# Rope attention and SoLU MLP on one core: the first tables and keys loaded and rotated in two column halves, with a new order of issue

## The chip, the cores and the metric

The kernel runs on one core of a Trainium2 chip. The metric is the device time of one execution in microseconds (us); the median of three timed runs stands for the kernel. A profile is taken of one further execution, and all rows below are of that one.

## The reference, cut to what matters

Rotary attention over 4 batches x 8 heads of 576 positions x 64, and then an MLP over the 2304 rows of 512 that the heads give together:

```
q_rot, k_rot = rotate(q), rotate(k)                      # x1*cos - x2*sin, x1*sin + x2*cos
attn = softmax(scale * q_rot @ k_rot.T) @ v              # per batch and head
h = x @ w_in                                             # 2304x512 @ 512x1024
solu = h * softmax(h);  ln = layernorm(solu) * g_ln
out = ln @ w_out                                         # 1024 -> 512
```

## The kernel before

**Tiling.** The 32 heads go as 16 pairs (P = 0 to 15): a pair's two heads lie in the two halves of the 128 partitions. `raw["k"]` and `raw["q"]` hold one pair as the chip loads it, 128 partitions x 2 planes x 576 columns: plane 0 is x, plane 1 is x with its halves swapped. The table `tabs` has the same shape (cosines, sines). A rotation is three operations (line 359, a helper that DVE or POOL runs): plane 0 times cosine, plane 1 times sine, and their sum into `rot`. Pairs 0 to 3 multiply `rot` in fp32; from pair 4 on each operand is split in a high and a low fp32r part, and the scores take three products.

**Stages of a pair.** `pair_tile(i)`, i = 0 to 3, makes the scores of 128 queries of both heads, called S P.i here (line 425), into two of the three two-bank buffers "D" of PSUM. Then `stats`: DVE takes the row maximum (line 405), ACT the exponential into `e` (line 407). The scores' buffer is free after the exponential. `turn_tile` transposes `e`, called T P.i.h for the head h: in pairs 0 to 3 on TensorE (line 489), from pair 4 on nearly always by DMA, out to `escr`, back into `e`, and then a DVE transposition in blocks into `ET` (line 510). `packed` makes the last 64 queries of both heads (S P.4, lines 452 to 461), and `av` multiplies with v (A P.r, line 564). After four pairs a batch is whole, and its 4 or 5 row tiles go through `front` (h, line 638) and `back` (o, line 711).

**The prologue** (`prologue`, line 729) loads table and pair 0 and rotates pair 0. The query goes in two column pieces, columns 0 to 191 first. `early` (line 721) issues matmuls without use on a constant tile: five of them ahead of the first scores, two after them. `weights` splits the two weight matrices in high and low parts (jobs w0 to w15, lines 809 to 828); its loads and operations lie among the first pairs.

**Order.** Every operation is added to a list with a number (`Plan.add`); `ORDER` is a hand-kept permutation of these numbers, and the program issues them in it. Every engine runs its own operations strictly in that order, and all loads and stores go through one queue, SP. `FLIP` holds the numbers of operations that run on their second engine (DVE in place of POOL or ACT, mostly, or POOL for DVE), `BUFS` the buffer of each use. Where an operation has to wait, all that stands behind it on its engine waits too.

The places that matter below, by the numbers of `ORDER`:

- Prologue: loads 12 to 18, rotations 23 to 33, first scores S 0.0 = 117.
- Pair 4: load of the pair-6 keys = 691 and queries = 692; `e` back from `escr` for T 4.0.1 = 702, its DVE transposition = 703.
- Pair 6: load of the pair-9 queries = 987; `e` back from `escr` for T 6.3.0 = 943, its DVE transposition = 944; the same two of T 6.0.1 = 899 and 900.

Of the kernel before, what the change touches and what calls it, by code (L numbers as in the profile page):

```python
# [32 lines left out]
    2, 12, 16, 13, 27, 14, 23, 17, 29, 15, 24, 3, 4, 5, 6, 7, 18, 26, 25, 28, 30, 32, 117, 126, 34, 38, 35,  # L33
    19, 31, 33, 118, 119, 127, 43, 44, 120, 36, 37, 39, 45, 47, 122, 123, 121, 1, 52, 53, 106, 128, 131,
    132, 20, 129, 130, 40, 124, 109, 125, 139, 140, 141, 108, 151, 154, 133, 56, 10, 155, 152, 46, 48, 135,
    107, 112, 134, 160, 136, 137, 163, 61, 158, 138, 153, 110, 142, 161, 9, 115, 143, 144, 49, 65, 111, 171,
    164, 172, 113, 54, 145, 146, 159, 70, 147, 148, 162, 55, 173, 41, 42, 149, 50, 179, 57, 116, 167, 168,
    201, 204, 114, 150, 62, 63, 58, 169, 170, 193, 205, 156, 174, 157, 175, 180, 202, 203, 210, 176, 178,
    177, 181, 182, 64, 165, 166, 79, 211, 206, 207, 213, 185, 214, 192, 208, 186, 209, 71, 72, 195, 196,
    197, 200, 194, 233, 234, 212, 221, 235, 222, 184, 183, 223, 236, 59, 187, 188, 217, 218, 51, 80, 66, 8,  # L40
    73, 237, 224, 242, 243, 244, 74, 215, 21, 216, 245, 189, 190, 238, 239, 75, 253, 81, 191, 254, 82, 240,
    246, 249, 67, 68, 83, 199, 60, 84, 88, 76, 283, 277, 250, 284, 241, 85, 225, 77, 219, 220, 278, 279,
    255, 227, 228, 229, 261, 262, 230, 231, 285, 286, 89, 263, 288, 69, 86, 90, 289, 226, 232, 287, 292,
    295, 251, 252, 97, 293, 296, 258, 260, 87, 78, 446, 247, 248, 294, 303, 98, 275, 282, 315, 318, 259,
    301, 302, 264, 290, 265, 256, 319, 324, 450, 267, 99, 257, 268, 291, 447, 274, 269, 270, 297, 100, 316,
    92, 327, 325, 328, 101, 266, 335, 304, 305, 298, 271, 448, 102, 198, 91, 276, 281, 272, 326, 329, 306,
    317, 336, 337, 330, 361, 373, 362, 93, 103, 104, 363, 364, 273, 456, 374, 320, 321, 343, 308, 280, 340,
    342, 341, 94, 486, 375, 376, 357, 105, 356, 307, 338, 339, 358, 371, 299, 377, 372, 300, 449, 382, 383,
    385, 457, 458, 359, 360, 322, 323, 95, 309, 96, 310, 22, 333, 334, 344, 345, 386, 311, 384, 312, 313,
    314, 346, 451, 452, 466, 393, 394, 395, 380, 396, 368, 405, 406, 487, 488, 348, 459, 489, 381, 347, 461,  # L50
    378, 460, 391, 379, 407, 331, 453, 408, 332, 392, 454, 414, 415, 417, 677, 409, 387, 388, 416, 350, 351,
    462, 418, 476, 349, 491, 389, 390, 490, 398, 676, 425, 463, 365, 693, 426, 427, 696, 697, 467, 682, 433,
    434, 694, 397, 681, 678, 468, 11, 477, 695, 399, 400, 401, 402, 492, 701, 403, 683, 493, 404, 528, 352,
    353, 354, 355, 470, 704, 419, 420, 410, 366, 411, 423, 496, 435, 529, 530, 691, 424, 478, 707, 705, 706,
    702, 412, 708, 494, 469, 471, 472, 479, 413, 531, 421, 436, 480, 717, 718, 500, 698, 481, 482, 495, 709,
    729, 730, 732, 692, 430, 699, 532, 679, 680, 703, 497, 498, 437, 684, 719, 367, 431, 712, 422, 499, 534,
# [12 lines left out]
    836, 819, 901, 640, 880, 889, 860, 861, 862, 809, 863, 562, 844, 563, 564, 881, 891, 892, 834, 902, 849,
# [874 lines left out]
```

## Time and profile before

| | |
|---|---|
| median of 3 runs | 445.88 us (445.01 to 448.03) |
| profiled execution | 447.05 us |
| its span, first to last instruction | 445.3 us |
| mean granted TensorE clock | 0.995 |
| busy: PE, DVE, ACT, POOL | 97%, 86%, 65%, 56% |
| moved by DMA | 109.29 MB, mean 245 GB/s |

A row of the timeline reads: start, duration, engine, line, operation, what it writes <- what it reads, shapes, count, and in brackets the engine's idle time before it and what ended that. PE is TensorE's matmuls, PEld its weight loads, SPq the issue of a DMA on the queue SP. A row of the windows gives the busy time of each engine in a stretch, the granted clock (1.00 is 2.4 GHz, 0.50 is 1.2 GHz), the busy share of the DMA engines and their rate.

### The profile page before, as it was taken

What the parts mean: (1) busy time and instruction counts of PE and PEld (TensorE: products, weight loads), DVE (VectorE), ACT (ScalarE), POOL (GpSimd) and SP (SyncE); (2) the same over time, 40 slices, a digit from 0 to 9 for tenths busy, and PEclk for the clock granted to TensorE, in tenths of its full rate; (3) what the DMA queues carried; (4) which work ended last, traced back from release to release, by engine and by line L of the source; (5) the groups of instructions that cost most, each with busy time, mean ns of one, the idle gap of its engine ahead of it and who ended that gap; (6) DMA issues with size and microseconds to landing.
All of it is one profiled execution on the core that took longest, in us unless ns stands there. A gap on an engine that the chain in (4) does not pass through costs nothing.

```text
span 445.3 us, 8147 instructions
## 1 busy us (share of the span) xinstructions
PE 431.1 (97%) x2658; PEld 312.9 (70%) x2658; DVE 382.7 (86%) x608; ACT 291.6 (65%) x646; POOL 250.2 (56%) x286
## 2 busy tenths in 40 slices
PE   7889999999999998999999999999999999999996
PEld 3465666777777685767677678777776776868885
DVE  3999989999999988888799899989899987865762
ACT  1989999999876764567465767576867545344431
POOL 2656766688889657375586577366747330303440
PEclk9999999999999998999999999999999999999999
DMA  7746575788899989998999999999999976534331
GB/s 254 270 164 217 167 222 178 234 257 298 248 311 306 266 263 277 296 282 248 321 315 275 292 346 288 295 302 283 270 282 292 311 223 214 173 106 165 118 142 48
DMA packets 93243, 109.29 MB, mean 245 GB/s; under 512 B 8464, under 2 KB 68752, under 8 KB 93200
## 3 DMA queue, kind: packets, MB, share of 16 engines
q1 hardware_dynamic: 93200, 108.76, 77.3%
q8 instruction: 21, 0.34, 0.3%
q14 instruction: 22, 0.18, 0.1%
HBM read 70.91 MB, written 37.82 MB: 244 GB/s over the span
## 4 chain that ended last, share of the span: by engine, by line
PE 71%; DMA 8%; DVE 5%; issue 4%; SPq 2%; POOL 2%; ACT 1%; DVEq 0%; POOLq 0%; ACTq 0%
PE pg L711 20%; PE pd L638 19%; PE pg L564 13%; PE pd L425 10%; PE pg L489 7%; DMA e<-escr 5%; PE pd L452 2%; DMA escr<-e 1%; DVE ET L510 1%; SPq L343 1%; DVE mx L405 1%; DMA wraw<-uscr 1%; PE pg L839 1%; DMA rscr<-rs 1%; POOL rawk L359 1%
## 5 line engine op out<-in xcount | busy, mean ns | idle before, releaser
L407 ACT ACTIVATE e<-pd,mx 128x576 f32<-128x576 f32 x132 | 97.4, 740 | 43.6 <-DVE mx L405 25.7
L510 DVE STREAM_TRANSPOSE ET<-e 128x512 f32<-128x512 f32 x90 | 99.7, 1132 | 5.6 <-DMA e<-escr 5.5
L405 DVE TENSOR_REDUCE mx<-pd 128x1 f32<-128x576 f32 x132 | 94.7, 742 | 9.8 <-PE pd L425 8.8
L564 PE MATMUL pg<-ET,vst 128*64 128x256 f32 (+1 forms) x512 | 70.4, 414 | 0.2 <-ACT ET L328 0.2
L703 POOL TENSOR_TENSOR lnl<-tb,lnh 128x512 fp32r<-128x512 f32 x26 | 33.7, 1297 | 46.7 <-ACT lnh L328 40.3
L638 PE MATMUL pd<-wih,xh 128*128 128x512 f32 x144 | 59.2, 411 | 0.0
L711 PE MATMUL pg<-woh,lnh 128*128 128x512 f32 x144 | 59.0, 410 | 0.0
L489 PE MATMUL pg<-idn,e 128*128 128x128 f32 (+1 forms) x308 | 54.7, 295 | 4.0 <-ACT EL L328 1.7
L489 PEld LDWEIGHTS pg<-idn,e 128*128 128x128 f32 (+1 forms) x308 | 40.8, 186 | 24.6 <-issue 6.4
L711 PE MATMUL pg<-woh,lnl 128*128 128x512 f32 x144 | 57.0, 396 | 0.0
L638 PE MATMUL pd<-wih,xl 128*128 128x512 f32 x144 | 56.9, 395 | 0.0
L711 PE MATMUL pg<-wol,lnh 128*128 128x512 f32 x144 | 56.9, 395 | 0.0
L638 PE MATMUL pd<-wil,xh 128*128 128x512 f32 x144 | 56.8, 395 | 0.0
L564 PEld LDWEIGHTS pg<-ET,vst 128*64 128x64 f32 x512 | 34.0, 137 | 24.9 <-issue 4.0
L693 DVE STREAM_TRANSPOSE tb<-wraw 128x512 f32<-128x512 f32 x36 | 38.4, 1096 | 1.1 <-DMA wraw<-uscr 1.1
L425 PE MATMUL pd<-kh,qh 64*128 64x288 f32 x192 | 34.7, 343 | 2.5 <-ACT e L407 1.6
L359 POOL TENSOR_TENSOR rawq<-rawq,tabs 128x576 f32<-128x576 f32 (+1 forms) x22 | 29.9, 1361 | 11.0 <-DMA rawq<-in_q_t_dram 10.8
L359 POOL TENSOR_TENSOR xl<-xT,xh 128x512 fp32r<-128x512 f32 x15 | 20.0, 1331 | 27.5 <-ACT xh L328 27.0
L328 ACT COPY ET<-pg 128x512 f32<-128x512 f32 x50 | 28.8, 584 | 9.9 <-PE pg L489 9.7
L359 POOL TENSOR_TENSOR rawk<-rawk,tabs 128x576 f32<-128x576 f32 x21 | 30.4, 1457 | 7.1 <-DMA rawk<-in_k_t_dram 7.0
L711 PEld LDWEIGHTS pg<-woh,lnh 128*128 128x128 f32 x144 | 27.1, 188 | 7.4 <-issue 1.8
L711 PEld LDWEIGHTS pg<-woh,lnl 128*128 128x128 f32 x144 | 27.1, 188 | 6.8 <-POOL lnl L703 0.3
(120 smaller groups left out, 891.9 us busy)
## 6 DMA issues: line engine op xcount, KB each, us to landing
escr<-e SPq DMA_DIRECT2D x90, 256.0 KB
e<-escr SPq DMA_DIRECT2D x90, 256.0 KB
uscr<-u SPq DMA_DIRECT2D x18, 512.0 KB
wraw<-uscr SPq DMA_DIRECT2D x18, 512.0 KB
rawk<-in_k_t_dram SPq DMA_DIRECT2D x15, 576.0 KB
rawq<-in_q_t_dram SPq DMA_DIRECT2D x15, 576.0 KB
vst<-in_v_t_dram SPq DMA_DIRECT2D x16, 320.0 KB
out_dram<-o SPq DMA_DIRECT2D x18, 256.0 KB
```

The lines of the kernel that those rows point to most:

```text
L328: nc.scalar.copy(o, i)
L359: add(*c[0], prio, lambda e: e.tensor_tensor(o, a, b, op=op), r, w, alt=c[1], two=True)
L405: add("dve", 672, t, lambda: nc.vector.tensor_reduce(mx[:, mcol:mcol + 1], buf(us)[:, :, 0:288], axis=AX.XY, op=ALU.max, negate=True), [sk ...
L407: add("act", 720, t, lambda: nc.scalar.activation(e.rearrange("p (z n) -> p z n", z=2), buf(us)[:, :, 0:288], AF.Exp, bias=mx[:, mcol:mcol ...
L425: nc.tensor.matmul(buf(us)[:, z, 0:288], a[rows, c0:c0 + 128], w[rows, 288 * z:288 * z + 288], start=(j == 0), stop=(j == len(terms) - 1))
L489: nc.tensor.transpose(dst, src, idn)
L510: add("dve", 1040, t, lambda: nc.vector.transpose(ET[r][:, h, :, q0:q0 + 128].rearrange("p m (a j) -> p j m a", j=4), e.rearrange("p (j b ...
L564: nc.tensor.matmul(buf(uy)[rows, 0:nq], vv[:, m, h, :], e, start=(m == 0), stop=(m == 4))
L638: nc.tensor.matmul(buf(uh)[:, z, :], a[:, c, :], w[:, c, HF * z:HF * z + HF], start=(c == 0 and j == 0), stop=(c == KC - 1 and j == 2))
L693: add("dve", 1050, tl, lambda z=z, turned=turned: nc.vector.transpose(turned().rearrange("p m (a j) -> p j m a", j=4), v[:, :, 128 * z:128 ...
L703: add(*c[0], tl, lambda e, hd=hd, ld=ld, turned=turned: e.tensor_tensor(ld, turned(), hd, op=ALU.subtract), [bk] + kl[0][z], kl[1][z], use ...
L711: nc.tensor.matmul(buf(uo), a[:, f, :], w[:, f, :], start=(f == 0 and j == 0), stop=(f == FC - 1 and j == 2))
```

## The change

Four edits of the code:

1. The table is loaded as two halves of columns (0 to 287, 288 to 575), each with both planes, and the keys of pair 0 likewise. Before, the table came as two planes, the keys as plane 0 whole and plane 1 in two halves. There are two loads of the table and two of the keys now, 1152 bytes in a row each; before two of the table and one of the keys with 2304 bytes in a row and two of the keys with 1152.
2. The keys are rotated in two halves of three operations each; before, plane 0 was multiplied in one operation of 576 columns.
3. S 0.0 is two operations, one for each half of the keys, and the first needs only the first half.
4. `ORDER`, `FLIP` and `BUFS` are replaced. Numbers from 118 on are one higher, since S 0.0 is two operations.

```diff
-        dma(-100, tabs[:, 0, :], tab[:, 0, :], nb, w=[("tab", 0)])
-        dma(-99, tabs[:, 1, :], tab[:, 1, :], nb, w=[("tab", 1)])
-        dma(-98.5, raw["q"][:, :, h0], q_t[0][:, :, h0], nb * 2 / 3, w=[("raw", "q", "a")])
-        dma(-98, raw["k"][:, 0, :], k_t[0][:, 0, :], nb, w=[("raw", "k", "c")])
         for z, x in enumerate(hs):
-            dma(-97, raw["k"][:, 1, x], k_t[0][:, 1, x], nb / 2, w=[("raw", "k", "s", z)])
+            dma(-100 + z, tabs[:, :, x], tab[:, :, x], nb, w=[("tab", z)])
+            if z == 0:
+                dma(-100, raw["q"][:, :, h0], q_t[0][:, :, h0], nb * 2 / 3, w=[("raw", "q", "a")])
+            dma(-99.5 + z, raw["k"][:, :, x], k_t[0][:, :, x], nb, w=[("raw", "k", "h", z)])
...
-        tt("dve", -80, a, a, tabs[:, 0, :], ALU.mult, S, [("raw", "k", "c"), ("tab", 0)] + kw, [("rp", "k", 0)])
         for z, x in enumerate(hs):
-            tt("dve", -79, s_[:, x], s_[:, x], tabs[:, 1, x], ALU.mult, S // 2, [("raw", "k", "s", z), ("tab", 1)] + kw, [("rp", "k", 1, z)])
-            tt("dve", -79, rot["k"][0][:, x], a[:, x], s_[:, x], ALU.add, S // 2, [("rp", "k", 0), ("rp", "k", 1, z)] + kw,
+            ky = [("raw", "k", "h", z), ("tab", z)] + kw
+            tt("dve", -79, a[:, x], a[:, x], tabs[:, 0, x], ALU.mult, S // 2, ky, [("rp", "k", 0, z)])
+            tt("dve", -79, s_[:, x], s_[:, x], tabs[:, 1, x], ALU.mult, S // 2, ky, [("rp", "k", 1, z)])
+            tt("dve", -79, rot["k"][0][:, x], a[:, x], s_[:, x], ALU.add, S // 2, [("rp", "k", y, z) for y in range(2)] + kw,
...
-            def S_op():
-                for z in range(2):
+            def S_op(zs=range(2)):
+                for z in zs:
...
+            if jt == 0:
+                for z in range(2):
+                    add("pe", 485, tau(P, 0) - 4, lambda z=z: S_op((z,)), [kk[z], q0k], sk + [("turn",)], use=(ua, ub), mode=1)
```

What the two lists say, read by operation and engine:

| place | before | after |
|---|---|---|
| SP, start | table plane 0, keys plane 1 first half, table plane 1, queries 0 to 191, keys plane 1 second half, keys plane 0, queries 192 on, w0, identity, w1, w2, keys of pair 1, v, queries of pair 1 | queries 0 to 191, table half 0, keys half 0, table half 1, keys half 1, queries 192 on, w0, identity, w1, keys of pair 1, queries of pair 1, w2, v |
| PE, start | 5 early, S 0.0, 2 early, T 0.0.0, S 0.1, T 0.0.1, S 0.2 | 5 early, S 0.0 in two, 2 early, S 0.1, T 0.0.0, T 0.0.1, S 0.2 |
| ACT, start | w0 (two operations), exponential S 0.0 first head, w1 (two), exponential S 0.0 second head | w0 (two), exponential S 0.0 first head, w1 (one), exponential S 0.0 second head, w1 (one) |
| SP, pair 4 | 691 (pair-6 keys), 702 (`e` of T 4.0.1), 2 stores and 4 small ones, 692 (pair-6 queries) | 692 (pair-6 keys), 693 (pair-6 queries), 703 (`e` of T 4.0.1) |
| DVE, pair 4 | maxima of S 4.2, transposition T 4.0.1, w13 (three operations) | maxima of S 4.2, w13 (three operations), transposition T 4.0.1 |
| SP, pair 6 | 987 (pair-9 queries), 943 (`e` of T 6.3.0) | 900 (`e` of T 6.0.1), 944 (`e` of T 6.3.0); 988 (pair-9 queries) stands later, see below |
| PE, S 6.3 to S 7.3 | the same operations but for one transposition that stands before or after five o products | |
| DVE, all | 590 operations of the list | 585 |
| PE, all | 638 operations of the list in 260 runs of one kind | 639 in 256 |

The lines of `ORDER` for pair 4 and pair 6 (not whole):

```diff
-    353, 354, 355, 470, 704, 419, 420, 410, 366, 411, 423, 496, 435, 529, 530, 691, 424, 478, 707, 705, 706,
-    702, 412, 708, 494, 469, 471, 472, 479, 413, 531, 421, 436, 480, 717, 718, 500, 698, 481, 482, 495, 709,
-    729, 730, 732, 692, 430, 699, 532, 679, 680, 703, 497, 498, 437, 684, 719, 367, 431, 712, 422, 499, 534,
...
-    919, 992, 987, 655, 973, 980, 953, 954, 1260, 960, 943, 600, 601, 961, 900, 886, 989, 990, 996, 999,
...
+    684, 405, 529, 530, 679, 692, 481, 480, 494, 411, 412, 356, 420, 421, 706, 424, 707, 425, 434, 693, 435,
+    413, 708, 709, 703, 436, 470, 472, 482, 718, 535, 536, 495, 414, 719, 720, 710, 370, 371, 431, 433, 501,
...
+    973, 960, 974, 975, 934, 651, 961, 937, 887, 1001, 993, 985, 1003, 900, 1002, 901, 944, 945, 1004, 1013,
+    1014, 585, 652, 653, 654, 655, 656, 600, 980, 1025, 657, 988, 1026, 994, 919, 976, 1027, 1261, 659, 921,
```

## Rows read from the trace of the kernel before

**Rows 1.** The page, part 1: busy time and instructions of every engine.
```profile
PE 431.1 (97%) x2658; PEld 312.9 (70%) x2658; DVE 382.7 (86%) x608; ACT 291.6 (65%) x646; POOL 250.2 (56%) x286
```

**Rows 2.** Windows, 20 to 100 us: PE, PEld, DVE, ACT, POOL, clock, DMA share, GB/s.
```profile
20.00:100.00 80.00, 76.39 (x533) 50.75 (x533) 76.76 (x142) 74.44 (x169) 52.99 (x40) 1.00 0.64 205
```

**Rows 3.** Timeline of the first 18 us: rotations, first scores, first maxima and exponentials.
```profile
6.14 0.46 DVE L359 TENSOR_TENSOR rawk<-rawk,tabs 128x288 f32<-128x288 f32 x1 [4.76 <-DMA tabs<-in_tab_dram]
...
6.76 1.38 POOL L359 TENSOR_TENSOR rawq<-rawq,tabs 128x192 f32<-128x192 f32 x2 [6.33 <-DMA rawq<-in_q_t_dram]
...
8.02 0.76 DVE L359 TENSOR_TENSOR rawk<-rawk,tabs 128x576 f32<-128x576 f32 x1 [0.32 <-DMA rawk<-in_k_t_dram]
8.22 1.00 POOL L359 TENSOR_TENSOR rotq<-rawq 128x192 f32<-128x192 f32 x1
8.81 1.10 DVE L359 TENSOR_TENSOR rotk<-rawk 128x288 f32<-128x288 f32 x2
...
9.68 1.24 PE L425 MATMUL pd<-rotk,rotq 64*128 64x288 f32 x8 [0.88 <-DVE rotk L359]
...
10.05 1.03 DVE L359 TENSOR_TENSOR rawq<-rawq,tabs 128x384 f32<-128x384 f32 x2
...
10.85 1.98 PE L725 MATMUL pg<-lnh 128*128 128x512 f32 x4
11.00 1.42 DVE L405 TENSOR_REDUCE mx<-pd 128x1 f32<-128x576 f32 x2
...
11.49 0.68 ACT L817 ACTIVATE wraw<-wraw 128x512 int32<-128x512 uint32 x1 [9.49 <-DMA wraw<-in_w_in_dram]
...
12.62 0.72 ACT L407 ACTIVATE e<-pd,mx 128x576 f32<-128x576 f32 x1
...
14.17 1.24 PE L425 MATMUL pd<-rotk,rotq 64*128 64x288 f32 x8
...
17.14 1.24 PE L425 MATMUL pd<-rotk,rotq 64*128 64x288 f32 x8 [0.97 <-ACT e L407]
```

**Rows 4.** Windows of 2 us, the first loads; columns as in Rows 2.
```profile
4.00:6.00 2.00, 2.00 (x4) 0.81 (x3) 0.00 (x0) 0.00 (x0) 0.00 (x0) 1.00 0.95 278
```

**Rows 5.** Waits of PE, 100 to 445 us: us in total, times, longest.
```profile
PE pd L425 <- ACT e L407: 1.6, 1, 1.6
```

**Rows 6.** Timeline, 159 to 170 us: queue SP, DVE and PE around T 6.3.0.
```profile
159.53 0.59 SPq L343 DMA_DIRECT2D rawq<-in_q_t_dram  x1
160.24 0.37 SPq L343 DMA_DIRECT2D e<-escr  x1
...
167.31 1.15 DVE L510 STREAM_TRANSPOSE ET<-e 128x512 f32<-128x512 f32 x1 [2.10 <-DMA e<-escr]
...
169.99 0.40 PE L425 MATMUL pd<-kh,qh 64*128 64x288 f32 x1 [1.55 <-ACT e L407]
```

**Rows 7.** Windows after that stall, and after the idle time at 17 us.
```profile
170.00:175.00 5.00, 5.00 (x31) 3.75 (x33) 3.83 (x8) 2.82 (x8) 3.29 (x3) 0.66 1.06 340
...
18.00:20.00 2.00, 1.55 (x12) 1.05 (x8) 1.93 (x6) 1.66 (x5) 1.53 (x2) 1.00 0.36 140
```

**Rows 8.** Timeline, 83 to 93 us: queue SP, POOL and DVE around T 4.0.1.
```profile
83.41 1.55 POOL L359 TENSOR_TENSOR rotq<-rawq 128x576 f32<-128x576 f32 x1 [0.69 <-DVE rawq L359]
...
84.04 0.33 SPq L343 DMA_DIRECT2D e<-escr  x1
...
88.23 0.45 SPq L343 DMA_DIRECT2D rawq<-in_q_t_dram  x1
...
91.55 1.13 DVE L510 STREAM_TRANSPOSE ET<-e 128x512 f32<-128x512 f32 x1
```

**Rows 9.** Groups by line and shape, DVE, 15 to 100 us: busy us, mean ns of one.
```profile
L359 DVE TENSOR_TENSOR rawk<-rawk,tabs 128x576 f32<-128x576 f32 x7 | 5.9, 849 | 0.0
L811 DVE TENSOR_SCALAR xT<-xT 128x512 f32<-128x512 f32 x9 | 5.6, 625 | 0.0
...
L359 DVE TENSOR_TENSOR wil<-xT,wih 128x512 fp32r<-128x512 f32 x3 | 2.4, 789 | 0.0
```

More of the change, by code (lines that the diff above doesn't have):

```diff
@@ L32 @@
 ORDER = [
[127 rows of a table removed]
[127 rows of a table added]
 ]
 FLIP = {
[5 rows of a table removed]
[5 rows of a table added]
 }
 BUFS = (
-    "0010002110002111100112011101002001021000201100101211011000211110101010121010200100211100002011101221"
-    "0200102011001000121001212101111012010202100001210100101010111102120110211011010012111220012001110210"
-    "2112011120021101102121112101010110220002021100011211010101010000020011121200200212112121101220101001"
-    "02210112101211020021020011121011020002010000002200112110200201200121010"
+    "0011002101001211200111011201010001020012100120001011211001011021100010112101010100201011102001011012"
+    "1102011011010100102012020002001211001101202100100211202001001021020101201111110010011010210202012101"
+    "2102010120200001001221112121120012002000201002110012111212112010011221200100201212100121101201002011"
+    "10020102211011001101110101120010110000112121011002100010101210201210011"
 )
@@ L370, in rope @@
             e = eng[p]
-            tt(e, prio, a, a, tabs[:, 0, c0:c1], ALU.mult, n, [rk[0], ("tab", 0)], [pk[0]])
-            tt(e, prio, s_, s_, tabs[:, 1, c0:c1], ALU.mult, n, [rk[1], ("tab", 1)], [pk[1]])
+            tk = [("tab", 0), ("tab", 1)]
+            tt(e, prio, a, a, tabs[:, 0, c0:c1], ALU.mult, n, [rk[0]] + tk, [pk[0]])
+            tt(e, prio, s_, s_, tabs[:, 1, c0:c1], ALU.mult, n, [rk[1]] + tk, [pk[1]])
             tt(e, prio, o, a, s_, ALU.add, n, pk + rk, wk)
@@ L766, in turn_q @@
             ky = [("raw", "q", y)] + qw
-            tt("dve", p, a, a, tabs[:, 0, c], ALU.mult, n, ky + [("tab", 0)], [("rp", "q", 0, y)])
-            tt("dve", p, s_, s_, tabs[:, 1, c], ALU.mult, n, ky + [("tab", 1)], [("rp", "q", 1, y)])
+            tk = [("tab", 0)] + ([("tab", 1)] if y == "b" else [])
+            tt("dve", p, a, a, tabs[:, 0, c], ALU.mult, n, ky + tk, [("rp", "q", 0, y)])
+            tt("dve", p, s_, s_, tabs[:, 1, c], ALU.mult, n, ky + tk, [("rp", "q", 1, y)])
             tt("dve", p, rot["q"][0][:, c], a, s_, ALU.add, n, [("rp", "q", 0, y), ("rp", "q", 1, y)] + qw, [("rot", "q", 0, "ab".index(y))])
```

3 lines of the change are left out of this document (2 added, 1 removed), and 256 rows, old and new, of tables (FLIP, ORDER).

## The prediction

> **What bounds the kernel now.** First the page's busy times: TensorE is busy for 97% of the span, DVE for 86% [rows 1]. So the kernel is worth what TensorE does not spend, 445.3 - 431.1 = 14.2 us of the span, and what it spends slowly. Then the windows say where that idle time lies. From 20 to 100 us, which is pairs 0 to 3 and the weights, PE is idle for 80 - 76.39 = 3.6 us, DVE for 3.2 us, ACT for 5.6 us [rows 2]: three engines are nearly full, so an operation handed to one of them can lengthen that stretch, and an earlier start is soon eaten by whichever is fullest. After 100 us PE's list of waits has one that matters, 1.6 us in one piece for an exponential [rows 5]. The timeline shows its whole chain [rows 6]: a load of raw queries of 576 KB is issued at 159.53, the load of `e` for T 6.3.0 behind it at 160.24; DVE idles for 2.10 us until that lands and transposes at 167.31; the maxima of S 7.2 stand behind it on DVE, their exponentials on ACT behind them, and S 7.3 needs the buffer that these free. PE idles for 1.55 us to 169.99. The windows then show the second price: from 170 to 175 us the mean granted clock is 0.66 [rows 7], so 0.34 x 5 = 1.70 us are lost at the lower level of 1.2 GHz. An idle time of 0.97 us ahead of 17.14 [rows 3] was followed by a clock of 1.00 [rows 7]. The one stall therefore cost 1.55 + 1.70 = 3.25 us.
>
> **The start, edits 1 to 3.** Before, DVE waited for table plane 1 to 6.14 and for keys plane 0 to 8.02 [rows 3]. Ahead of the one and with it the queue had 288 + 144 + 288 = 720 KB, up to the other 1344 KB: 624 KB in 1.88 us, 332 KB a us. By the new order queries and both first halves make 768 KB, so the first keys are there at 6.14 + 48 / 332 = 6.28, and the table's first half (480 KB) at 5.42. All 1344 KB are still there at 8.02. POOL's query rotation took from 6.76 to 9.22, 2.46 us [rows 3], and now ends at 5.42 + 2.46 = 7.88. Three half operations on DVE take 0.46 + 0.46 + 0.55 = 1.47 us (0.55 is half of the 1.10 of the two sums): the first half is rotated at 7.75, the second at 8.02 + 1.47 = 9.49, where before it was 9.91. The early matmuls end at 9.68 - 0.88 = 8.80; the first part of S 0.0 follows at once and takes half of 1.24, 0.62; the second part starts at 9.5 and ends at 10.1, in place of 10.92. So the first scores are 0.8 us sooner. DVE then has the two query operations (1.03) and starts the first maximum at 10.5 rather than 11.00, 0.5 us sooner. There it ends: ACT runs two operations of w0 first, which waited for their load to 11.49, and the first exponential comes at 12.62, after them [rows 3]; the new order leaves these two ahead of it, and the bytes ahead of w0 are the same. What the order adds is that the second exponential stands ahead of one operation of w1 (0.68 sooner) and S 0.1 ahead of T 0.0.0: at 13.4, when the first exponential is done, rather than at 14.17. Bounds 0 to -0.8 us; ACT is the nearest limit and has 5.6 us of idle time in the next 80 [rows 2], so I take -0.3.
>
> With S 0.1 there, PE's two early matmuls end at 10.1 + 1.98 = 12.1 and PE idles for 1.3 us to 13.4, more than the 0.97 that kept the clock and less than the 1.55 that lost it. Price 0 to 1.7; I take 0, because here PE waits for ACT anyway.
>
> w2's load and that of v move behind both loads of pair 1, which wait for the rotations of pair 0; v is multiplied only with the first `av`, after four scores, and w2's operations stand later on ACT as well. I cost both at nothing; uncovered, it would be the 0.68 of one ACT operation.
>
> **Smaller pieces.** Rows of 2304 bytes become 1152: on average over these loads 1344 KB go from 896 to 1280 rows, 1536 to 1075 bytes. With 0.95 of the DMA engines' time used they moved 278 GB/s [rows 4]. From below: from 170 to 175 us, with stores of `e` in pieces of 512 bytes among the traffic, 340 GB/s were moved [rows 7], so a shorter piece need not cost. From above: if the rate fell with the length of a piece, the about 4.1 us of transfer to 8.02 grow by 0.43, +1.8 us. I take +0.3, near the row with the 512-byte pieces.
>
> The Trainium skill, Perfetto Trace Analysis, section DMA Optimizations, speaks against this edit: transfers under 2 KB are said to carry significant overhead, and splitting to start sooner is advised where the DMA engines are generally idle, which at a share of 0.95 they are not. By it the upper bound of the sentence before would stand, and the sum below would be 445.0.
>
> **The engines in pairs 0 to 3 (`FLIP`).** Up to S 4.0 DVE gains four rotation operations and loses one, net 3 x 0.849; it loses four clippings of weights to POOL, 4 x 0.625; copies out of PSUM nearly cancel, and two operations of w2 come to it, at most 2 x 0.789 [rows 9]. That is +0.05 to +1.6 us on an engine with 3.2 us of idle time in 80 [rows 2]. A gain is excluded here, since none of the engines loses work that PE waited for. I take +0.5.
>
> **Pair 6.** PE's operations from S 6.3 to S 7.3 are the same but for one exchange, and DVE still has the transposition of T 6.3.0 ahead of the maxima of S 7.2. But its load no longer stands behind 576 KB of raw queries; the load of `e` for T 6.0.1, 256 KB, stands ahead of it instead. So 320 KB less: at 278 GB/s [rows 4], the slowest rate in these rows, 1.2 us sooner. DVE's wait falls from 2.10 to 0.9, PE's from 1.55 to 0.35, which is below the 0.97 that kept the clock. Saved: 1.2 + 1.7 = 2.9 us; bounds 0 (the transfer was late for another reason) and 3.25. I take 2.9.
>
> **Sum.** -0.3 + 0.3 + 0.5 - 2.9 = -2.4 us. The profiled execution took 447.05 (span 445.3 and 1.75 around it), 1.17 over the median of the three runs; I carry that difference over: 447.05 - 2.4 = 444.65 profiled, and 445.88 - 2.4 = 443.5 as a median. The rest of the order, more than two thousand operations, is read as even: the PE list changes its kind of product 255 times in place of 259, and its other stalls before were small [rows 5].
>
> **The rivals.** (1) The stall in pair 6 stays, or one like it comes elsewhere. For it: the transposition still stands ahead of the maxima, and the DMA engines are full there (1.06) [rows 7]. Against: less is queued ahead. 445.88 + 0.5 = 446.4. (2) Slower: the load of `e` for T 4.0.1 lands late. Before, it was issued at 84.04, with the pair-6 queries behind it at 88.23, and DVE transposed at 91.55 without a wait [rows 8]. Now the pair-6 queries stand ahead of it; they need their buffer, which POOL's sum holds to 83.41 + 1.55 = 84.96, and they are 590 KB, 2.1 us at 278 GB/s. So the load lands some 3 us later, while DVE comes to it only about 1.9 us later (three operations of w13, an estimate by the 0.625 of one such [rows 9]). It decides if the load before landed after about 91.55 + 1.9 - 3 = 90.4; then DVE waits, with the maxima of S 4.3 behind it, and if PE's idle time passes the 0.97 us that kept the clock, the price is that of the stall at 168, 3.25: 443.5 + 3.3 = 446.8. The same step in another pair would cost as much again. (3) All of it: the start brings its 0.8 and the 0.7 of S 0.1, the stall goes whole, DVE's extra work is hidden: 445.88 - 0.8 - 0.7 - 3.25 = 441.1. (4) The shorter pieces cost their upper bound, 1.8 in place of 0.3, for which the DMA share of 0.95 speaks [rows 4] and against which the 340 GB/s do [rows 7]: 443.5 + 1.5 = 445.0. This is the rule of the Trainium skill named above, in Perfetto Trace Analysis.
>
> **How the numbers follow.** Forecast 0.37, (1) 0.25, (2) 0.17, (3) 0.13, (4) 0.08. The predicted time is 443.5. The forecast's own range is 442.5 to 444.9. All but (2) with a second or third late load lie between 440.8 and 448.8, and I leave out 0.08 below and 0.10 above, for orders that stall twice more or lose the small waits between 20 and 100 us. About 1%, 4.5 us, is what a measurement here can tell from no change: faster, under 441.4, has most of (3), 0.12; slower, over 450.3, is (2) twice over, 0.08; within 1% the rest, 0.80.
>
> **What would show it.** In the profile after: first part of S 0.0 at about 8.8, the second ending near 10.1, the first exponential still near 12.6 behind w0; no stall of PE over 1 us ahead of S 7.3 and a clock of 1.00 after it; T 4.0.1 on DVE without an idle time of over 1 us. The prediction is wrong if the clock falls in a new place, if w0 lands over half a us later, or if the stretch from 20 to 100 us has more than 4.5 us of PE idle time.

## The result, and the profile of the changed kernel

The changed kernel takes 450.03 us (median of 17 runs, 446.89 to 455.26) beside 446.73 us (17 runs, 444.78 to 452.85) of the kernel before: a ratio of 1.0072, with a 95% interval of 1.0047 to 1.0098. It is slower by 0.7%, about 3.2 us. Forecast were 443.5 us and a range that ends at 448.8. In the band of 1% that the prediction calls no change the result still lies, but its sign and its size are wrong. The profiled execution took 450.73 us (span 448.9, mean clock 0.991; before 445.3 and 0.995).

The windows of the profile after say which stretch it is; the columns are those of [rows 2].

```profile
0.00:20.00 20.00, 16.35 (x56) 8.31 (x58) 12.55 (x26) 9.23 (x19) 6.26 (x17) 1.00 0.81 271
20.00:100.00 80.00, 73.12 (x481) 47.86 (x480) 74.22 (x133) 67.44 (x154) 54.31 (x38) 0.96 0.63 191
...
58.00:62.00 4.00, 4.00 (x20) 2.19 (x22) 4.00 (x8) 3.77 (x10) 1.36 (x1) 0.57 0.62 213
88.00:92.00 4.00, 1.32 (x9) 0.89 (x8) 3.97 (x6) 1.17 (x3) 2.50 (x3) 1.00 0.81 245
92.00:96.00 4.00, 3.72 (x13) 2.77 (x13) 2.66 (x8) 3.73 (x10) 2.32 (x2) 0.57 0.79 256
```

From 20 to 100 us PE is now idle for 6.9 us, where [rows 2] have 3.6, and the granted clock is 0.96 in place of 1.00: in two stretches of 4 us it stands at 0.57, between the two levels of 1.2 and 2.4 GHz and near the lower one. Each of the two stretches follows a stall of PE, one that ends at 57.98 and one that ends at 90.86 (both shown below). From 88 to 92 us one can see who is not waiting: DVE is busy for 3.97 of 4 us, while PE and ACT stand nearly still. The timeline of that stretch shows with what DVE is busy (some of PE's, DVE's and POOL's lines, in order of time and not all of them; "<-" names what ended the idle time).

```profile
83.31 3.94 POOL L817 TENSOR_SCALAR xT<-xT 128x512 f32<-128x512 f32 x2
...
87.21 0.32 POOL L359 TENSOR_TENSOR qzl<-rotq,qzh 64x64 fp32r<-64x64 f32 x1
87.28 3.12 DVE L819 TENSOR_SCALAR xT<-xT 128x512 uint32<-128x512 uint32 x1 [0.47 <-POOL xT L817]
87.49 1.40 POOL L359 TENSOR_TENSOR rotq<-rawq 128x576 f32<-128x576 f32 x1
88.85 1.26 POOL L359 TENSOR_TENSOR xl<-xT,xh 128x512 fp32r<-128x512 f32 x1
90.32 0.48 DVE L574 TENSOR_TENSOR xT<-pg,Rb 128x320 f32<-128x320 f32 x1
90.86 0.97 PE L494 MATMUL pg<-idn,e 128*128 128x128 f32 x6 [2.50 <-DVE xT L574]
```

Each block of weights goes through a few operations: ACT takes its absolute value, then it is clipped between two bounds, and then its bits are shifted and masked. L817 is the clipping (line 811 before), which DVE or POOL can run; L819 is the shift that reads it, which always runs on DVE. POOL clips two blocks until 87.25. DVE stands at the shift of block w11 and waits 0.47 us for it. Then the shift, 0.43 us by itself (measured below), takes 3.12 us, to the end of three operations that POOL runs without a gap. Behind it in DVE's queue is the multiplication of A 2.1, which frees the PSUM buffer that PE needs: PE waits for 2.50 us, and the clock falls. At 58 us it is the same with block w7 (timeline, 52 to 58 us):

```profile
52.05 2.42 POOL L817 TENSOR_SCALAR xT<-xT 128x512 f32<-128x512 f32 x1
...
54.45 1.40 POOL L359 TENSOR_TENSOR rotk<-rawk 128x576 f32<-128x576 f32 x1
54.51 1.63 DVE L819 TENSOR_SCALAR xT<-xT 128x512 uint32<-128x512 uint32 x1 [0.47 <-POOL xT L817]
...
56.33 0.73 DVE L406 TENSOR_REDUCE mx<-pd 128x1 f32<-128x576 f32 x1
...
57.09 0.74 ACT L408 ACTIVATE e<-pd,mx 128x576 f32<-128x576 f32 x1 [1.90 <-DVE mx L406]
...
57.98 0.53 PE L463 MATMUL pd<-rotk,rotq 64*64 64x288 f32 x1 [1.77 <-ACT e L408]
```

Here a norm and the maximum of S 2.2 stand behind the shift, the exponential behind the maximum, and the next scores behind the exponential. The groups by line give the sums (busy us, mean ns of one, idle us before): seven clippings are on POOL, one was before, and the shifts became longer without any change of their own.

```profile
L817 POOL TENSOR_SCALAR xT<-xT 128x512 f32<-128x512 f32 x7 | 14.3, 2042 | 5.4 <-ACT xT L815 5.3
L819 DVE TENSOR_SCALAR xT<-xT 128x512 uint32<-128x512 uint32 x12 | 11.9, 995 | 1.5 <-POOL xT L817 1.4
```

The same groups in the trace of before:

```profile
L811 POOL TENSOR_SCALAR xT<-xT 128x512 f32<-128x512 f32 x1 | 2.1, 2070 | 4.1 <-ACT xT L809 4.1
L813 DVE TENSOR_SCALAR xT<-xT 128x512 uint32<-128x512 uint32 x12 | 5.4, 452 | 0.1
```

At the start the steps came in the order forecast, with other times (timeline of after; [rows 3] has those of before):

```profile
9.04 0.82 DVE L359 TENSOR_TENSOR rawk<-rawk,tabs 128x288 f32<-128x288 f32 x2 [1.27 <-DMA rawk<-in_k_t_dram]
10.41 0.76 PE L426 MATMUL pd<-rotk,rotq 64*128 64x288 f32 x4 [0.97 <-DVE rotk L359]
...
12.85 0.72 ACT L408 ACTIVATE e<-pd,mx 128x576 f32<-128x576 f32 x1
...
13.81 1.24 PE L426 MATMUL pd<-rotk,rotq 64*128 64x288 f32 x8 [0.73 <-ACT e L408]
```

The stall of [rows 6] in pair 6 is gone: from 160 to 180 us PE is busy throughout. T 4.0.1, the second rival's place, caused no wait: DVE came to it at 99.94 and began at once.

That the two stalls are no accident of one execution shows in the mean granted clock of every execution. Two stretches of 4 us at 0.57 lose 2 x 0.43 x 4 = 3.4 us, which makes a mean of 0.992 over a span of 449 us. All 17 executions of the changed kernel have 0.996 or less, and 13 of them 0.992 or less. Of the 81 timed executions of the kernel before, in the three groups of runs below, 60 have 0.998 or more.

### The profile page after: what moved, and what is told of

Its sections match the earlier page's. It is cut to its first block, busy times and chain, and to the rows that moved or that the text cites. A ratio compares the mean times of both kernels' runs of the same rounds, so it can differ in the third digit from the quotient of the medians.

```text
span 448.9 us, 8162 instructions
## 1 busy us (share of the span) xinstructions
PE 433.3 (97%) x2658; PEld 313.4 (70%) x2658; DVE 384.8 (86%) x603; ACT 289.8 (65%) x644; POOL 265.4 (59%) x294
## 4 chain that ended last, share of the span: by engine, by line
PE 69%; DMA 11%; DVE 6%; ACT 3%; issue 2%; SPq 2%; POOL 1%; DVEq 0%; POOLq 0%
PE pg L716 20%; PE pd L643 19%; PE pg L569 12%; PE pd L426 9%; PE pg L494 5%; DMA escr<-e 4%; DMA e<-escr 3%; DVE mx L406 2%; SPq L343 2%; PE pd L457 2%; DMA Rb<-rscr 2%; DMA rscr<-rs 1%; ACT e L408 1%; DVE ET L515 1%; DMA rawk<-in_k_t_dram 1%
## 5 line engine op out<-in xcount | busy, mean ns | idle before, releaser
L569 PE MATMUL pg<-ET,vst 128*64 128x320 f32 (+1 forms) x512 | 70.8, 416 | 0.5 <-ACT EL L328 0.4
L708 POOL TENSOR_TENSOR lnl<-tb,lnh 128x512 fp32r<-128x512 f32 x28 | 36.1, 1293 | 44.0 <-ACT lnh L328 32.0
L359 POOL TENSOR_TENSOR rawq<-rawq,tabs 128x576 f32<-128x576 f32 (+1 forms) x25 | 34.8, 1397 | 5.8 <-DMA tabs<-in_tab_dram 4.6
L359 POOL TENSOR_TENSOR xl<-xT,xh 128x512 fp32r<-128x512 f32 x14 | 18.0, 1286 | 28.2 <-PE pg L716 14.5
L359 POOL TENSOR_TENSOR rawk<-rawk,tabs 128x576 f32<-128x576 f32 x20 | 28.8, 1451 | 7.7 <-DMA rawk<-in_k_t_dram 7.5
L426 PE MATMUL pd<-kh,qh 64*128 64x288 f32 x192 | 33.3, 343 | 0.0
L643 PEld LDWEIGHTS pd<-wih,xl 128*128 128x128 f32 x144 | 27.3, 190 | 7.6 <-POOL xl L359 1.0
```

What stands on the lines that cost most here:

```text
L359: add(*c[0], prio, lambda e: e.tensor_tensor(o, a, b, op=op), r, w, alt=c[1], two=True)
L426: nc.tensor.matmul(buf(us)[:, z, 0:288], a[rows, c0:c0 + 128], w[rows, 288 * z:288 * z + 288], start=(j == 0), stop=(j == len(terms) - 1))
L569: nc.tensor.matmul(buf(uy)[rows, 0:nq], vv[:, m, h, :], e, start=(m == 0), stop=(m == 4))
L643: nc.tensor.matmul(buf(uh)[:, z, :], a[:, c, :], w[:, c, HF * z:HF * z + HF], start=(c == 0 and j == 0), stop=(c == KC - 1 and j == 2))
L708: add(*c[0], tl, lambda e, hd=hd, ld=ld, turned=turned: e.tensor_tensor(ld, turned(), hd, op=ALU.subtract), [bk] + kl[0][z], kl[1][z], use ...
```

## The experiments

Every run was timed in turn with the kernel before on the same chip (medians of before 446.6, 446.75 and 446.4 us in the three groups of runs); the ratios are to it. In the kernels with an edited list the line numbers stand up to 8 higher, since the lists wrap differently. The first theory (C) was: POOL's clippings are the loss. Against it stood: the new start (S), and the order as such (O).

**The changed kernel, six clippings back on DVE.** The six that POOL has more than before (w2, w6, w7, w9, w10, w11), the order unchanged:

```diff
 FLIP = {
-    54, 90, 99, 459, 469, 479
```

> The changed kernel with the six clippings of weights (jobs w2, w6, w7, w9, w10, w11) back on DVE, nothing else undone. Theory C (the clippings on POOL are the loss: each takes 1.9 us there in place of 0.4, and the DVE operation behind it then waits for POOL): the PE stalls of 1.77 us at 58 and 2.50 us at 91 are gone with their stretches at half clock, some 7 to 8 us of the profile; time 0.985 to 0.99 of the kernel before in the same runs. Theory O (the new order as a whole stalls PE in pairs 0 to 3, whoever clips): PE idles for over 6 us from 20 to 100 us as in the changed kernel (6.9), ratio 1.004 to 1.010.

Measured: 450.32 us, ratio 1.0102 (1.0057 to 1.0147). The clock is 1.00 from 20 to 100 us, but PE is idle there for 8.7 us. PE still waits, for 1.45 us at 58.6 and for 2.26 us at 88.6. These are the signs of O, not of C: nothing was won. The undoing isn't clean, though: the list has a clipping where POOL could begin it, and on DVE it now stood ahead of maxima and waited for ACT (3.7 us in three waits).

**The kernel before, the same six clippings on POOL.**

```diff
 FLIP = {
+    54, 90, 99, 458, 468, 478
```

> The kernel before with those six clippings on POOL, nothing else changed. Theory C: at least one PE stall of over 1.5 us between 30 and 100 us that the kernel before does not have, and a stretch at half clock behind it; ratio 1.006 to 1.02. Theory O: the old order bears it, ratio 0.998 to 1.003.

Measured: 451.68 us, ratio 1.0144 (1.0096 to 1.0192), PE idle for 7.2 us from 20 to 100 us, and the clock 0.96. PE waits for 2.77 us at 60.2 and for 2.07 us at 91.5, C's sign, and the first of these has the same chain (timeline, 56 to 61 us):

```profile
56.28 1.62 DVE L814 TENSOR_SCALAR xT<-xT 128x512 uint32<-128x512 uint32 x1 [1.81 <-POOL xT L812]
...
60.16 0.45 PE L459 MATMUL pd<-rotk,rotq 64*64 64x288 f32 x1 [2.77 <-ACT e L408]
```

In the old order this one change of engine costs 6.4 us, by the medians about twice what the whole change did. So clippings on POOL can make the loss; whether they do it in the new order, the two runs leave open.

**The kernel before with the new start.** The loads, rotations and first scores of the change; order, engines and buffers behind them as before:

```diff
-    2, 12, 16, 13, 27, 14, 23, 17, 29, 15, 24, 3, 4, 5, 6, 7, 18, 26, 25, 28, 30, 32, 117,
+    2, 13, 12, 22, 14, 25, 26, 27, 23, 24, 3, 15, 16, 29, 4, 5, 6, 7, 117, 28, 30, 17, 32, 118,
```

> The kernel before with the new start alone: table and keys in column halves, S 0.0 in two operations, the head of the list of issue (up to the first scores) as in the changed kernel; behind it the old order, engines and buffers. The prediction's working: between -0.8 us and +1.8 us, ratio 0.998 to 1.004. If the start is what costs (theory S): the last keys land a us later than before, the first exponential comes 0.2 us or more later, and the ratio is that of the changed kernel, 1.007.

Measured: 445.06 us, ratio 0.9973 (0.9947 to 1.0000). S falls: the 1.007 of the changed kernel lie outside the interval, so the part that the change is named for is not what costs. Whether it brings anything isn't shown. The middle of the interval is 1.2 us, but its end is no change, and the traces show no gain behind the start: S 0.3 begins at 19.79 to 20.46 us in three profiled executions with the old start (the kernel before, the run above and the next one), and at 19.95 to 20.60 in three with the new start and the old order behind it (this run and the two crossed ones below that keep the old first half).

**The kernel before, T 6.3.0's load ahead of the queries of pair 9.**

```diff
-    919, 992, 987, 655, 973, 980, 953, 954, 1260, 960, 943,
+    919, 992, 943, 987, 655, 973, 980, 953, 954, 1260, 960,
```

> The kernel before with one exchange in the queue: the load of e for T 6.3.0 ahead of the raw queries of pair 9. The prediction's step for pair 6: DVE's wait of 2.10 us is gone or under 1 us, PE does not idle over 1 us near 168, the clock stays at 1.00, 2.9 us saved, ratio 0.993 to 0.995. Rival: the load is late for another reason (DMA engines full), the stall stays, ratio 0.999 to 1.001.

Measured: 446.34 us, ratio 0.9994 (0.9963 to 1.0025). The stall of [rows 6] is gone from the trace and the time is the same: the 2.9 us of the prediction lie outside this interval. The rival's ratio came, without its mechanism. In the run with the new start nothing was touched there, and yet DVE waits for this load for 0.38 us in place of 2.10, and PE's stall is gone (160 to 180 us: 19.74 us of PE). In the first of the crossed runs below, untouched there too, DVE waits 1.09 us and PE 0.56, and the clock stays at 1.00. The transposition of T 6.3.0 in these three traces, this run first, then the new start and the crossed run:

```profile
165.51 1.15 DVE L517 STREAM_TRANSPOSE ET<-e 128x512 f32<-128x512 f32 x1
...
166.07 1.16 DVE L522 STREAM_TRANSPOSE ET<-e 128x512 f32<-128x512 f32 x1 [0.38 <-DMA e<-escr]
...
169.23 1.18 DVE L523 STREAM_TRANSPOSE ET<-e 128x512 f32<-128x512 f32 x1 [1.09 <-DMA e<-escr]
```

So how late the load is differs from one execution to the next, and one profile in which the stall is gone can't show that the exchange took it away. The clocks of all executions say how often the full price was paid: the 1.70 us lost at the lower level make a mean clock of 0.996, and 60 of the 81 executions of the kernel before have 0.998 or more, as 8 of the 12 of this run have. The stall with its whole price was in a minority of the executions.

**The two halves of the order, crossed.** The list was cut ahead of the first score of pair 4. First the new list up to there and the old one behind it:

> The changed kernel's order, engines and buffers up to the first score of pair 4 (430 operations), behind it those of the kernel before. Theory H (the loss is made in pairs 0 to 3): about as slow as the changed kernel, 449 to 451, PE idle for 6 us or more from 20 to 100 us, and the clock below 1.00 there. Rival R (the loss is made behind pair 4, and what is seen ahead of it is made up for): about 445 to 446.5, as the kernel before with the new start alone.

Measured: 447.6 us, ratio 1.0029 (1.0000 to 1.0058). The wait of 1.77 us at 58 is there, that at 90 isn't; PE is idle for 4.7 us from 20 to 100 us, at a clock of 1.00. The time lies between the two theories. Then the old list, with the new start, and the new one behind:

> The other way round: the new start, then the order, engines and buffers of the kernel before up to the first score of pair 4, behind it those of the changed kernel. Theory H: about 444 to 446, PE idle for about 4 us from 20 to 100 us and the clock 1.00 there; if the new rest is worth something by itself it comes out below the 445.06 of the new start alone. Rival R: 449 to 451.

Measured: 450.29 us, ratio 1.0099 (1.0068 to 1.0130), with the clock at 0.96 and PE idle for 8.3 us from 20 to 100 us. The time is R's, the stalls are not where R has them. Both theories were too coarse: beside the 0.9973 of old and old, each half costs something. The trace shows why H fails for the second run: the stall at 90 belongs to the new list's first microseconds behind the cut, and here it is worse (timeline).

```profile
86.60 3.11 DVE L826 TENSOR_SCALAR xT<-xT 128x512 uint32<-128x512 uint32 x1 [1.82 <-POOL xT L824]
...
89.63 0.48 DVE L581 TENSOR_TENSOR xT<-pg,Rb 128x320 f32<-128x320 f32 x1
...
90.16 1.55 PE L501 MATMUL pg<-idn,e 128*128 128x128 f32 x6 [4.13 <-DVE xT L581]
```

So there are two places, one in each half, and at both DVE stands at the shift of a block that POOL clips.

**The clippings on DVE, directly ahead of their shifts.** A cleaner form of the first run (the same engines, and for example):

```diff
-    427, 366, 390, 491, 391, 492, 493, 468, 469, 351, ... 436, 470, 472,
+    427, 366, 390, 491, 391, 492, 493, 468, 351, ... 436, 469, 470, 472,
```

> The changed kernel, its six clippings back on DVE as in the run with the clippings undone, but each issued directly ahead of the shift that reads it, so that DVE waits for no other engine at a new place. Theory C' (clippings on POOL are the loss, and the run that undid them stalled only because DVE came to them too early): 444.5 to 446.5, clock 1.00 from 20 to 100 us, PE idle for about 4 us there. Rival O (the rest of the order of pairs 0 to 3 stalls by itself): 448 to 450, PE idle for 7 us or more there.

Measured: 448.35 us, ratio 1.0043 (1.0013 to 1.0073). That time is rival O's; PE is idle for 6.8 us, just under its 7, and only the clock of 1.00 is as C' said. PE still waits for 1.5 us at 57.6 and for 1.6 us at 88.2. Ahead of A 2.1's multiplication DVE now has a clipping of 1.49 us and a shift of 0.43. At w7's place DVE waits for no clipping, and the shift still takes 1.51 us, beside a sum of POOL:

```profile
53.97 1.46 POOL L366 TENSOR_TENSOR rotk<-rawk 128x576 f32<-128x576 f32 x1 [4.58 <-PE pg L501]
54.21 1.51 DVE L826 TENSOR_SCALAR xT<-xT 128x512 uint32<-128x512 uint32 x1
...
57.56 0.45 PE L470 MATMUL pd<-rotk,rotq 64*64 64x288 f32 x1 [1.52 <-ACT e L415]
```

Which engine clips is only a part of it; another part is that work on weights stands ahead of what PE waits for. That gave theory D, and its test.

**One shift later.** The clippings stay on POOL. Of the whole list one operation moves, the shift of w11 (480), to just ahead of its reader:

```diff
-    684, 405, 529, 530, 679, 692, 481, 480, 494, 411, 412, 356, ... 436, 470, 472, 482,
+    684, 405, 529, 530, 679, 692, 481, 494, 411, 412, 356, ... 436, 470, 472, 480, 482,
```

> The changed kernel with one operation moved: DVE's shift of weight block w11 goes behind A 2.1's multiplication, two maxima of S 4.1, and three operations of norms, to just ahead of the one operation that reads it. The clippings stay on POOL. Theory D (the loss at 88 to 96 us is this shift at the head of DVE's queue, waiting for POOL and then shut out by it, with the multiplication behind it that PE waits for): PE's wait of 2.50 us at 90.9 gone or below 0.9, the clock 1.00 from 92 to 96, and 2.5 + 1.7 = 4.2 us less: about 446. Rival E (POOL's load is what counts, and another DVE operation is shut out in its place): the wait comes again within some us, 449 to 450.

Measured: 447.58 us, ratio 1.0017 (0.9987 to 1.0047). The wait at 90.9 is gone and from 20 to 100 us the clock is 1.00. By the ratios it brought 2.5 us where 4.2 were expected; the two ratios come from different groups of runs, and with their intervals the 2.5 can be anything from about 0.7 to 4.2. The wait at 58 stays, and here the clock does not fall behind it (timeline, and the window of 58 to 62 us):

```profile
57.60 0.45 PE L470 MATMUL pd<-rotk,rotq 64*64 64x288 f32 x1 [1.77 <-ACT e L415]
...
58.00:62.00 4.00, 4.00 (x33) 2.22 (x30) 4.00 (x9) 3.77 (x10) 1.68 (x2) 1.00 0.50 162
```

**Two shifts later.** The shift of w7 (100) as well:

```diff
-    302, 253, 92, 291, 99, 100, 304, ... 363, 325, 277, 326, 328, 102,
+    302, 253, 92, 291, 99, 304, ... 363, 325, 277, 326, 328, 100, 102,
```

> As the run with one shift later, and the shift of w7 too goes behind the norm of pair 2 and three maxima of S 2.2 and S 2.3, to just ahead of its reader. Theory D: PE's wait of 1.77 us at 58 and the half clock behind it go as well: 1.8 + 1.6 = 3.4 us less than with one shift, bounded by what DVE lacks anyway: 443 to 445. Rival E: the stall at 58 stays at 1 us or more, and the time is that of one shift.

Measured: 444.55 us, ratio 0.9960 (0.9930 to 0.9989). Another 2.5 us by the ratios (about 0.7 to 4.4), and inside the 443 to 445 expected: two operations of some 2,350, moved by a few places, turn 0.7% slower into 0.4% faster. This version beats both kernels. Windows of its trace (clock and idle time at the two places, and one later stretch):

```profile
20.00:100.00 80.00, 75.96 (x518) 50.47 (x518) 77.08 (x139) 71.84 (x163) 57.96 (x42) 1.00 0.63 197
...
58.00:62.00 4.00, 4.00 (x31) 2.12 (x32) 3.96 (x8) 3.04 (x8) 2.86 (x4) 1.00 0.70 210
88.00:92.00 4.00, 3.84 (x26) 2.90 (x27) 3.90 (x8) 4.00 (x11) 2.98 (x3) 1.00 0.91 276
92.00:96.00 4.00, 4.00 (x20) 3.33 (x20) 3.83 (x10) 2.11 (x6) 1.31 (x1) 1.00 0.91 297
180.00:200.00 20.00, 18.12 (x110) 13.30 (x110) 15.81 (x26) 9.84 (x24) 8.32 (x8) 0.93 0.92 282
```

The last line shows where a part of the gain may go. In the profiled executions of this run and of the one with one shift later (1.81 us at 195.6), but not in the changed kernel's (180 to 200 us: PE 19.45, clock 1.00), PE waits later on, behind a transposition that waits for its load (timeline of the run with two shifts later):

```profile
192.59 2.11 DVE L522 STREAM_TRANSPOSE ET<-e 128x512 f32<-128x512 f32 x2 [2.32 <-DMA e<-escr]
...
196.59 0.63 PE L501 MATMUL pg<-idn,e 128*64 128x128 f32 x4 [1.88 <-ACT ET L335]
```

DVE comes to this transposition 4.1 us sooner than in the changed kernel (190.27 against 194.39), its load lands only 2.1 us sooner (192.59 against 194.71), and the clock falls to 0.93 over these 20 us. That fall alone would make a mean clock of 0.997, and nine of the twelve executions of this run have 0.999 or 1.000: in most of them the clock is not lost there. Whether PE waits there at full clock isn't shown, since only one execution of each run was profiled. The profiled execution of the run with two shifts is also the longest of its twelve (449.33 us): PE waited for 2.49 us ahead of S 0.1, since w0 had landed late, and the clock was 0.55 and 0.60 from 16 to 20 us.

**The old first half, and the new second one with the shift of w11 later.** The edit of the run with one shift, in the second of the crossed kernels:

> New start, pairs 0 to 3 as in the kernel before, the new order behind, and in it the shift of w11 moved as in the run with one shift later. Theory D: the wait of 4.13 us at 90.2 goes below 1 and the clock is 1.00 there; 450.3 - 4.1 - 1.7, so about 444.5, and PE idle for about 4 us from 20 to 100 us. Rival E: 448 or more.

Measured: 446.81 us, ratio 0.9999 (0.9971 to 1.0027), 0.0100 below the crossed kernel without the edit, or 4.5 us. The wait of 4.13 us is gone; PE is idle for 6.0 us from 20 to 100 us, not for 4, and it comes out 2.3 us above the expectation. Over the three runs with shifts moved the wait went each time, as D says, and each time the gain was smaller than the wait and its clock added up: 2.5 of 4.2, 2.5 of 3.4 and 4.5 of 5.8 us.

**DVE beside POOL, by itself.** No part of the reference is computed in the three runs that follow, and each was executed once.

> No part of the reference is computed: stages of eight DVE operations, alone or beside four POOL operations back to back, the output is zeros. Theory P (POOL shuts DVE out of SBUF while it runs, whichever DVE operation it is): the shift of 128x512, the clipping and the two-operand operations take 1.3 us or more each beside POOL, in place of 0.42 to 0.75 alone, the maximum out of PSUM stays at 0.74. Rival Q (DVE only loses turns, a few tenths each): the shift stays below 0.8. A clipping alone on POOL: 1.9 to 2.1 us, an subtraction of 128x512 alone 1.2 to 1.4.

> No part of the reference is computed: stages of eight DVE operations beside one to four POOL subtractions that follow each other at once, each into a tile of its own, the output is zeros. In the first such run, where POOL's operations wrote one tile and 0.08 us lay between them, one DVE shift got in after each (1.37 us a shift). Theory T (what is shut out waits for the end of the whole train when POOL's operations overlap): the first shift takes about 1.4, 2.7, 4.0 and 5.2 us beside one, two, three and four subtractions. Rival V (a turn after each POOL operation, so the 3.12 us in the changed kernel had another cause): no shift over 1.8 us in any stage.

The second of them, by line (duration in ns: shortest, median, longest; first and last start), for eight shifts alone, eight beside four subtractions, eight beside four clippings, and the maxima out of PSUM beside four subtractions:

```profile
L346 DVE TENSOR_SCALAR xT<-xT x8: 418/427/428, 5.8 to 9.0; 128x512 uint32<-128x512 uint32 x8
...
L346 DVE TENSOR_SCALAR xT<-xT x8: 426/898/1391, 24.3 to 31.3; 128x512 uint32<-128x512 uint32 x8
...
L346 DVE TENSOR_SCALAR xT<-xT x8: 427/708/808, 60.6 to 65.4; 128x512 uint32<-128x512 uint32 x8
...
L359 DVE TENSOR_REDUCE xT<-pd x8: 748/757/757, 53.9 to 59.4; 128x1 f32<-128x576 f32 x8
```

The first run shows the same: a shift waits out one whole subtraction of POOL (1.26 us alone, 1.37 to 1.47 for the shift), the DVE operations with two operands go from 0.69 and 0.76 to 1.66 and 1.72, and the maximum is not touched. P holds for subtractions. Beside clippings it doesn't: a shift takes at most 0.81 us, though a clipping keeps POOL for 1.91. And no shift was longer than 1.47, so V holds, and the 3.12 us were not explained. The third run put POOL's operations there as they stand in the kernel:

> No part of the reference is computed: trains of POOL operations in the shapes that ran beside the shift of 3.12 us (two 64x64, the sum of 128x576, the subtraction of 128x512 into the rounded type), with and without a clipping ahead that the shift waits for; six DVE shifts beside each; the output is zeros. Theory T' (a shift that starts when POOL's train is already under way waits for the whole train, and a short operation at its head makes that happen): about 3.1 us for the first shift where the 64x64 stands ahead, below 1.6 where it doesn't. Rival V' (one turn after each POOL operation, here too): no shift over 1.8 us, and the 3.12 us stay unexplained.

The timeline of one train: a clipping just ahead, the 64x64 subtraction, the sum, the 128x512 subtraction.

```profile
19.23 0.31 POOL L378 TENSOR_TENSOR qzl<-rotq,qzh 64x64 fp32r<-64x64 f32 x1
19.30 5.41 DVE L346 TENSOR_SCALAR xT<-xT 128x512 uint32<-128x512 uint32 x6 [1.72 <-POOL xT L391]
19.50 1.39 POOL L381 TENSOR_TENSOR rotq<-rawq 128x576 f32<-128x576 f32 x1
20.86 1.25 POOL L388 TENSOR_TENSOR wil<-woh 128x512 fp32r<-128x512 f32 x1
```

The shifts of both trains by line, as above:

```profile
L346 DVE TENSOR_SCALAR xT<-xT x6: 426/427/3100, 19.3 to 24.3; 128x512 uint32<-128x512 uint32 x6
...
L346 DVE TENSOR_SCALAR xT<-xT x6: 426/427/1612, 35.5 to 39.9; 128x512 uint32<-128x512 uint32 x6
```

The longest of six is the first. With the short operation at the head (first line) it takes 3.10 us, without it (second line) 1.61; over all trains it is 3.02 to 3.10 us in the three with the short operation and 1.37 to 1.61 in the three without. T' holds but for the hundredth by which 1.61 passes its 1.6, and a train of these operations is enough for the 3.12 us.

## Why the prediction was wrong

The sum was -0.3 (start) + 0.3 (pieces) + 0.5 (engines) - 2.9 (pair 6). At 446.5 us the runs put these beside it: the start with its pieces -1.2 (0 to -2.4), pair 6 -0.3 (+1.1 to -1.7), and the two shifts +5.0 in two steps of 2.5. That makes +3.5; measured are +3.2. The intervals of these terms are 2.4 to 3.4 us wide, so that they meet this closely is partly luck.

**The engines, +0.5, is the step that failed,** and with it the sentence that reads the rest of the order as even, which put the place of DVE's shifts at nothing. The step weighed busy times: so many clippings off DVE at 0.625 us, so much onto it. Six went over, five of them ahead of S 4.0, not the four that it counts. And what it left out decided:

- On POOL a clipping takes 1.91 to 2.42 us, and the trace of before had one row of it (2070 ns, shown above) that the step didn't use.
- The shift stays on DVE, so DVE now waits for POOL in the middle of its own queue: 1.4 us in all at the shifts, where it was 0.1 before.
- The shift then has to get past whatever POOL runs next: 1.63 and 3.12 us in place of 0.42.
- What counts is what is queued behind it. The step names no such operation; it asks only whether an engine loses work that PE waited for, which excludes a gain, and not whether PE would come to wait for what is added.

In its place the runs showed two shifts with PE's work behind them. PE waits for 1.77 and 2.50 us, the clock falls to 0.57 for 4 us twice, and moving the two shifts, with all the clippings still on POOL, brings 5.0 us (about 3.3 to 6.7). In the profile the same places cost 1.77 + 2.50 + 3.4 = 7.7 us; over all executions they cost less. How much of it is the engine's and how much the order's, the runs don't divide: the clippings on POOL cost 6.4 us in the old order, but taking them back in the new one, even at the best place tried, still left 1.0043.

As the forecast's own list of signs has it ("if the clock falls in a new place", "more than 4.5 us of PE idle time" from 20 to 100 us), both came true: 0.57 in two places, and 6.9 us.

**Pair 6, -2.9, was read from one execution.** The load did stand behind 576 KB, and the stall is gone from the profiles of the changed kernel and of the run with the exchange. But with the old order there it came whole in one profiled execution only, at a third of its length in another, and not in two more (PE busy for 19.74 and 20.00 of the 20 us from 160 on), so that the move took it away isn't shown. The mean clocks say that most executions of the kernel before did not pay its price. The step took the price off the median too ("I carry that difference over"), whose runs need not contain it. The rate in this step, 278 GB/s, is also not the slowest of its rows: 205 and 140 stand there, at DMA shares of 0.64 and 0.36; it is the slowest among those near full use. With this term alone at -0.3 the sum would have been 446.1.

**The start came near its forecast partly by luck.** The first half went as worked out: the keys rotated at 7.77 (forecast 7.75), the first part of S 0.0 at 8.69 (8.8). The second half did not: S 0.0 ends at 11.17 in the profile after (forecast 10.1, before 10.92), and over nine profiled executions with the new start at 10.61 on average, over three with the old one at 10.68. So the 0.8 us of the first scores did not come. The first exponential stood at 12.85 behind w0 (near 12.6). The cause is the second half's keys, and the price of smaller pieces is not settled: the second half's keys were there at 9.04 against 8.02, 1.0 us later and not 0.3. In six other profiled executions with the new start they came between 8.29 and 8.80, in two they were there by 7.82 and 7.99 without a wait; in the three with whole planes they came between 7.39 and 8.02. That is about 0.7 us, where the prediction took 0.3 and had 1.8 as its bound. The Trainium skill (Perfetto Trace Analysis, DMA Optimizations) says that DMAs under 2 KB have a significant overhead per transfer. The split loads here are 288 KB each, in rows of 1152 bytes, and the page doesn't say whether it means rows; the last keys did come later, while the start as a whole was no slower (0.9973, to 1.0000).

**The idle time ahead of S 0.1, priced at nothing,** was 0.73 us in the profile after and didn't cost the clock. In the first crossed run it was 2.31 and the clock held too (1.00 to 30 us), in the run with two shifts 2.49, and it fell.

**The rivals.** The second has the right kind, a late operation on DVE with the maxima behind it, a PE stall and a lower clock, and twice of it was its price for slower; its place and cause (T 4.0.1's load) were not. No rival had a wait of one engine for another over weights, though the prediction costed that very move.

**What the rest of the order brought** was read as even. With the two shifts out of the way the changed kernel is at -1.8 us, and its start alone at -1.2. So the reading failed at the two shifts; what remains of the order beside them differs from nothing by less than the intervals.

The Trainium skill (SBUF — State Buffer, section Who interferes with whom) has a rule that bears on this change. DVE and GpSimd (POOL) share a pair of ports. A DVE instruction in a mode that uses two ports, which `tensor_scalar` (the shift) can enter, contends with GpSimd for it, and whichever issues first holds it for its whole instruction while the other is blocked; a DVE instruction with two inputs in SBUF contends with one of GpSimd that reads SBUF; `tensor_reduce` (the maximum) never contends. No row shows in which mode the shift runs. The traces agree for subtractions (shift 1.37 to 1.47 beside 1.26, maximum 0.757 either way). They differ for a clipping on POOL (shift 0.43 to 0.81, median 0.71, beside 1.91), and 3.10 us are more than one instruction.

## What to carry to other kernels

When an operation moves to another engine, don't add up busy times: look at its reader. If the reader stays behind, its engine now waits in the middle of its queue, and everything behind it waits too; move the reader down to just ahead of its own reader. Taking the operation back to its old engine won none of the time back here, or a part of it (1.0102 and 1.0043 against 1.0072); moving the two readers won all of it (0.9960). And before a stall of one profiled execution is put into a sum against a median, see whether another execution has it; the mean clock of every execution tells how often its price was paid.

## What was not expected of the hardware

- A DVE shift of 128x512 (0.43 us) beside POOL's subtractions of 128x512 takes 1.37 to 1.47 us, one for each subtraction. Beside POOL's clippings, which are longer (1.91), it takes 0.43 to 0.81.
- With an operation of 0.31 us at the head of POOL's train, the shift was passed over by the two that followed: 3.02 to 3.10 us in three trains by themselves, and 3.12 and 3.11 in two kernels. Without it 1.37 to 1.61 in three trains. Why the short one makes the difference stays open.
- The clock is not lost by the length of a stall alone: the wait of 1.77 us at 58 was followed by 0.57 in the changed kernel, and by 1.00 in the run with one shift later, after the same wait of 1.77 at 57.6.
